# Channel chunks of four neighbours in every twenty, two exponential scales in one operation, and the last output rows on SyncE's queue

## The chip, the core and the metric

The kernel runs on one core of a Trainium2 chip. The core has five engines that run side by side and meet through semaphores: TensorE (PE in the profile; its weight loads are PEld), VectorE (DVE), ScalarE (ACT), GpSimd (POOL) and SyncE (SP), which here only issues transfers. ACT and POOL issue transfers too. The metric is the time on the device in microseconds (us) of one execution, and the median of several runs is compared.

## What is computed

Two independent layers stand side by side in the output (2048 positions, 640 + 640 columns), all in bfloat16.

```python
# A: attention over 8 keys at distances 0, 2, ..., 14; 32 heads of 20 columns
q, k, v = split(x @ wqkv)
a = softmax(scale * q . k[pos - 2 * w]) @ v[pos - 2 * w] @ wo
# B: a state-space layer (S4): 640 channels d, 192 states n, length 2048
dt = exp(log_dt)
P = exp(dt * (A_re + 1j * A_im) * l)                 # (d, n, l)
K = einsum("dn,dnl,dn->dl", C, P, dt * B).real       # one filter per channel
y = irfft(rfft(pad(u)) * rfft(pad(K)))[:2048] + u * Dskip
out = concatenate([a, y], axis=-1)
```

## The kernel before

Part B is built in five chunks of 128 channels (`NCH` = 5, the loop over c in `body`). A partition of a parameter tile stands for a channel of each chunk. The 640 channels are written as four groups g, in each of them 32 rows (u, t) with u of 4 and t of 8, and in each row five neighbours c: channel = 160 g + 40 u + 5 t + c. Chunk c takes every fifth channel. In the tiles that `partB_prep` loads, partition 32 u + 8 g + t holds a row of five channels, one for each chunk. `load` brings each parameter (B_A_re, B_A_im and four more) in with four transfers, one for each u, in which every partition's part is one run of 5 x 192 values. `ldt` is the logarithm of the step, `dtb` its exponential, `dtc` a float32 copy that scales the parameters on DVE. `alpha`, a float32 tile of 192 values for each partition and chunk, is the decay exponent that `decays` makes.

For each chunk, `exps_chunk` makes the powers exp(m x alpha): 14 in RA (m = 1 to 7 and 8 to 56) and 31 in RX (m = 64 to 64 x 31), one ACT operation for each m, and POOL fills the entries with m = 0. `phase_table` makes phases on PE and takes their sines on ACT (tiles TA and TX). `small_half` (L306 in the profile) multiplies powers and phases on DVE into PG, Q and X; `y_form` (L336) makes Y; `kgen_unit` multiplies X and Y on PE (L349 and L354), and one ACT copy (L355) stores eight filter rows in Ksb. A chunk has four such units. `transform` gives the filter's 32 rows of the chunk to `fwd`, a forward transform of length 4096 in two steps, each in four blocks of eight rows: PE (L368), evacuation on ACT (L369), PE (L375), evacuation on ACT (L376). `fwd_u` does the same for the input U, which lies in SBUF as 64 positions x 160 channels for each partition. `products` multiplies the two spectra on DVE (L400), `inverse_a` does half of the inverse (PE L416, ACT L417) and writes to memory (Zdram).

`times_d` (L430) multiplies U by the skip weights Dsb on DVE, 1024 elements at a time, ten times over the loop; the result lies in UD, a tile with one buffer, and POOL issues its transfer to memory (L431). `exps_chunk` is called for the chunk ahead, and `issue_after` queues its ACT operations behind the last sine.

Part A follows while the last chunk ends: projections and logits on PE, products on DVE, a softmax on ACT and DVE. In the last stage the sums over values and the output projection run on PE beside the second half of B's inverse (`Inverse.part`, whose copy writes the channels in order into ysb; SP sends them, L761). `out_piece` makes sixteen pieces of A's output; its transfers (L716) go in turn through POOL and SP, those of the last two pieces through SP. The scheduler of the framework orders the instructions of each engine, except where `keep_in_program_order` or `issue_after` pins them; every engine works its queue in order. The framework adds drains and a barrier at the end (L1061).

Of the kernel before, what the change touches and what calls it, by code (L numbers as in the profile page):

```python
# [16 lines left out]
NCH = 5  # L17
# [78 lines left out]
def partB_prep(tc, pools, prm):  # L96
# [15 lines left out]
    ldt = pl.tile([128, NCH], bf16, name="ldt")  # L112
    lsrc = prm["B_log_dt"].rearrange("(g u t c) -> u g t c", g=4, u=4, t=8)
# [3 lines left out]
    for u in range(4):  # L117
        late((nc.scalar, nc.sync)[u % 2].dma_start(out=ldt[32 * u:32 * u + 32, :], in_=lsrc[u]))
# [3 lines left out]
    def load(nm):  # L122
        nat[nm] = (pl if nm == "B_A_re" else pd).tile([128, NCH, 192], bf16, name=nm, tag=nm)
        src = prm[nm].rearrange("(g u t c) n -> u g t (c n)", g=4, u=4, t=8)
        for u in range(4):
            queue = {"B_A_re": (nc.scalar, nc.sync)[u % 2], "B_A_im": nc.gpsimd, "B_B_im": nc.gpsimd, "B_C_im": nc.gpsimd, "B_C_re": (nc.gpsimd, nc.sync)[u // 2]}.get(nm, nc.sync)
            late(queue.dma_start(out=nat[nm][32 * u:32 * u + 32].rearrange("p c n -> p (c n)"), in_=src[u]))
# [11 lines left out]
    dtb = pl.tile([128, NCH], bf16, name="dtb")  # L139
    late(nc.scalar.activation(out=dtb[:], in_=ldt[:], func=ACT.Exp))  # L140
    dtc = pl.tile([128, NCH], f32, name="dtc")
    V.tensor_copy(out=dtc[:], in_=dtb[:])
# [93 lines left out]
def exps_chunk(tc, pools, B, c):  # L236
    nc = tc.nc
    flat = pools["tab"].tile([128, 9216], bf16, name="R", tag=f"R{c % 2}")
    RA = flat[:, 0:3072].rearrange("p (h g q a f) -> p h g q a f", h=2, g=2, a=8, f=4)
    RX = flat[:, 3072:9216].rearrange("p (q e f) -> p q e f", e=32, f=4)  # L240
    al = B["alpha"][:, c]
    by_half = al.rearrange("p (h v) (q f) -> p h (v q) f", h=2, f=4)
    src = al.rearrange("p u (q f) -> p (u q) f", f=4)
    nc.gpsimd.memset(flat[:, 0:3072].rearrange("p (x a f) -> p x a f", a=8, f=4)[:, :, 0, :], 1.0)
    nc.gpsimd.memset(RX[:, :, 31, :], 1.0)
    for e, m in enumerate(R_MULT):
        if m == 0.0:
            continue
        if e < 16:
            nc.scalar.activation(out=RA[:, :, e // 8, :, e % 8, :], in_=by_half, func=ACT.Exp, scale=m)  # L250
        else:
            nc.scalar.activation(out=RX[:, :, e - 16, :], in_=src, func=ACT.Exp, scale=m)  # L252
    return RA, RX
# [171 lines left out]
def times_d(tc, pools, C, UDd, c, i):  # L425

    nc = tc.nc
    U = C["U"][:].rearrange("p l (ut c) -> p c l ut", c=NCH)[:, c]
    UD = pools["tabb"].tile([128, 32, 32], bf16, name="UD", tag="UD")
    tc.keep_in_program_order(nc.vector.tensor_tensor(out=UD[:], in0=U[:, 32 * i:32 * i + 32], in1=bc(C["Dsb"][:, c], 1, 32), op=A.mult))  # L430
# [3 lines left out]
def fwd_u(tc, pools, C, c, place):  # L434

    U = C["U"][:].rearrange("p l (ut c) -> p c l ut", c=NCH)[:, c]
    return fwd(tc, pools, C, (lambda ut: U[:, :, ut]), 0, pools["fft"], place)

# [5 lines left out]
class Attention:  # L444
# [251 lines left out]
    def out_piece(self, rows, last=False):  # L696
# [4 lines left out]
        whole = self.nop % 2 == 1 and not last  # L701
        self.nop += 1
# [12 lines left out]
        for k in range(ns):  # L715
            (nc.gpsimd, nc.sync)[last or k % 2].dma_start(out=self.out_a[512 * (s0 + k) + i0:512 * (s0 + k) + i0 + ni, :], in_=ob[ni * k:ni * k + ni])  # L716
# [5 lines left out]
class Inverse:  # L722
# [22 lines left out]
    def part(self, half, lo, n):  # L745
# [12 lines left out]
        self.att.copy(out=ysb[:, lo:lo + n].rearrange("p l (ut c) -> p l ut c", c=NCH), in_=ps[:, 0:160 * n].rearrange("p (l c ut) -> p l ut c", l=n, c=NCH))  # L758
# [8 lines left out]
def body(tc, ctx, pools, prm, B_u, B_Dskip, Sd, Zd, UDd, A_x, A_wqkv, A_wo, out_a, out_b):  # L767
# [14 lines left out]
    with tc.tile_pool(name="prep_l", bufs=1) as pl, tc.tile_pool(name="prep_d", bufs=1) as pd, tc.tile_pool(name="prep_g", bufs=1) as pg, tc.tile_pool(name="prep_h", bufs=1) as ph, tc.tile_pool(name="psum_p", bufs=2, space=bass.MemoryType.PSUM) as psp:  # L782
# [22 lines left out]
        nc.gpsimd.tensor_copy(out=Dsb[:], in_=Dn[:].rearrange("p (ut c) -> p c ut", c=NCH))  # L805
# [7 lines left out]
    def transform(c):  # L813
        Sk[c] = fwd(tc, pools, C, (lambda ut: Kb[c][:, ut, :]), 1, fp, "sa" if c == LAST else "ss")[0]
# [251 lines left out]
```

## Time and profile before

| | us |
|---|---|
| runs, median of 3 (lowest to highest) | 410.48 (408.87 to 410.54) |
| the profiled execution, its own time | 406.19 |
| its span, first to last instruction | 404.4 |

The granted TensorE clock of the profiled execution was 0.94 of full speed. A row of a group gives the line, the engine, the operation, the tiles (written from read), their shapes and the count, then the busy time, the mean time of one in nanoseconds, and the idle time of the engine just ahead with what ended it. A row in order of time gives the start, the duration in us, the engine and the same names, and in square brackets the idle time ahead of it. A queue has a q behind the engine's name (SPq).

### The profile page before, as it was taken

What the parts mean: (1) busy time and instruction counts of PE and PEld (TensorE: products, weight loads), DVE (VectorE), ACT (ScalarE), POOL (GpSimd) and SP (SyncE); (2) the same over time, 40 slices, a digit from 0 to 9 for tenths busy, and PEclk for the clock granted to TensorE, in tenths of its full rate; (3) what the DMA queues carried; (4) which work ended last, traced back from release to release, by engine and by line L of the source; (5) the groups of instructions that cost most, each with busy time, mean ns of one, the idle gap of its engine ahead of it and who ended that gap; (6) DMA issues with size and microseconds to landing.
All of it is one profiled execution on the core that took longest, in us unless ns stands there. A gap on an engine that the chain in (4) does not pass through costs nothing.

```text
span 404.4 us, 18790 instructions
## 1 busy us (share of the span) xinstructions
PE 347.6 (86%) x8565; PEld 261.4 (65%) x8565; DVE 369.6 (91%) x350; ACT 311.5 (77%) x572; POOL 58.1 (14%) x116
## 2 busy tenths in 40 slices
PE   1279769989898799987989999999989999779992
PEld 0267668877786788866788666656765677335651
DVE  7999998899998999999999799997967899899960
ACT  2996998789999999999999875633787545856661
POOL 8771000000010000100001000100010030221330
PEclk9975957999999799989998999999999999999997
DMA  5599003032035001440019644300564254697652
GB/s 151 165 233 196 6 3 132 31 74 63 29 131 129 10 6 54 123 118 3 3 60 195 131 99 105 122 11 3 211 162 105 90 146 115 210 248 224 199 137 56
DMA packets 40743, 43.36 MB, mean 107 GB/s; under 512 B 24144, under 2 KB 34096, under 8 KB 40024
## 3 DMA queue, kind: packets, MB, share of 16 engines
q1 hardware_dynamic: 35672, 30.36, 30.1%
q0 software_dynamic: 4848, 11.68, 9.7%
q8 instruction: 67, 1.10, 1.1%
q10 hardware_dynamic: 144, 0.12, 0.1%
q14 instruction: 12, 0.10, 0.1%
HBM read 19.69 MB, written 14.16 MB: 84 GB/s over the span
## 4 chain that ended last, share of the span: by engine, by line
PE 41%; ACT 38%; DVE 11%; issue 4%; DMA 2%; SPq 1%; ACTq 0%; DVEq 0%
ACT R L252 9%; ACT A L369 7%; PE ps_q L545 5%; PE ps_k L527 4%; ACT R L250 4%; PE ps_ph L277 4%; ACT A L376 4%; PE ps_v L558 4%; PE ps_k L349 4%; PE ps_k L354 3%; PE ps_f L375 3%; ACT Z L417 3%; DVE X L306 2%; PE ps_x L461 2%; DVE Y L336 2%
## 5 line engine op out<-in xcount | busy, mean ns | idle before, releaser
L336 DVE TENSOR_TENSOR Y<-PG 128x3072 bf16<-128x3072 bf16 x60 | 103.0, 1754 | 5.3 <-PE ps_k L354 5.3
L349 PE MATMUL ps_k<-Y,X 128*32 128x64 bf16 x1920 | 47.7, 239 | 8.0 <-DVE Y L336 4.1
L277 PE MATMUL ps_ph<-LPB,LPA 128*64 128x256 bf16 x320 | 35.4, 325 | 13.7 <-DMA LPA<-lo 8.2
L349 PEld LDWEIGHTS <-X 128*32 128x32 bf16 x1920 | 32.8, 117 | 18.6 <-issue 9.5
L376 ACT CAST A<-ps_f 128x1024 bf16<-128x1024 f32 x40 | 37.6, 1029 | 6.9 <-PE ps_f L375 6.9
L354 PE MATMUL ps_k<-Y,X 64*32 64x64 bf16 x1920 | 42.1, 233 | 0.0
L252 ACT ACTIVATE R<-LPB 128x192 bf16<-128x192 f32 x155 | 41.7, 377 | 0.0
L369 ACT CAST A<-ps_f 128x1024 bf16<-128x1024 f32 x40 | 37.7, 1040 | 0.6 <-PE ps_f L368 0.6
L306 DVE TENSOR_TENSOR X<-R,TX 128x1536 bf16<-128x1536 bf16 x40 | 37.6, 960 | 0.0
L375 PE MATMUL ps_f<-A,T 128*64 128x128 bf16 x640 | 28.6, 254 | 8.6 <-ACT A L369 8.6
L354 PEld LDWEIGHTS <-X 64*32 64x32 bf16 x1920 | 29.4, 112 | 7.8 <-issue 0.6
L375 PEld LDWEIGHTS <-T 128*64 128x64 bf16 x640 | 26.6, 126 | 10.3 <-issue 9.1
L668 DVE TENSOR_TENSOR prod<-v,atp 128x1536 bf16<-128x1536 bf16 (+3 forms) x32 | 30.8, 1023 | 1.2 <-ACT v L462 1.2
L285 ACT ACTIVATE TX<-ps_ph 128x768 bf16<-128x768 int16 x40 | 30.0, 840 | 0.9 <-PE ps_ph L281 0.7
L277 PEld LDWEIGHTS <-LPA 128*64 128x64 bf16 x320 | 18.4, 125 | 18.3 <-DMA LPA<-hi 8.3
L285 ACT ACTIVATE TA<-ps_ph 128x768 bf16<-128x768 int16 x40 | 29.6, 818 | 0.2
L578 DVE TENSOR_TENSOR prod<-qT,kT 128x1024 bf16<-128x1024 bf16 (+1 forms) x16 | 22.9, 1483 | 4.2 <-ACT qT L546 4.2
L281 PE MATMUL ps_ph<-LPB,LPA 128*64 128x128 bf16 x320 | 24.2, 248 | 0.0
L368 PE MATMUL ps_f<-BD,U 128*64 128x128 bf16 x320 | 20.7, 285 | 2.8 <-ACT Z L417 1.9
L527 PE MATMUL ps_k<-xT,wkq 128*128 128x512 bf16 x100 | 22.9, 379 | 0.2 <-ACT A L376 0.2
L545 PE MATMUL ps_q<-xT,wkq 128*128 128x512 bf16 x100 | 22.6, 379 | 0.0
L368 PEld LDWEIGHTS <-U 128*64 128x64 bf16 x320 | 19.6, 204 | 3.6 <-issue 3.0
(157 smaller groups left out, 719.1 us busy)
## 6 DMA issues: line engine op xcount, KB each, us to landing
P<-A SPq DMA_DIRECT2D x16, 256.0 KB
Zdram<-Z SPq DMA_DIRECT2D x16, 256.0 KB
Z<-Zdram SPq DMA_DIRECT2D x30, 128.0 KB
U<-in_B_u_dram SPq DMA_DIRECT2D x4, 640.0 KB
UDdram<-UD POOLq DMA_DIRECT2D x10, 256.0 KB, 2.8
out_dram<-ysb SPq DMA_DIRECT2D x32, 80.0 KB
Z<-UDdram SPq DMA_DIRECT2D x16, 128.0 KB
Z<-Zdram POOLq DMA_DIRECT2D x10, 128.0 KB, 4.6
```

The costliest lines, as they stand in the source:

```text
L252: nc.scalar.activation(out=RX[:, :, e - 16, :], in_=src, func=ACT.Exp, scale=m)
L277: MM(o[64 * hh:64 * hh + 64, :, 0:8], lhsT=L[:, 64 * hh:64 * hh + 64], rhs=rhs, start=first, stop=last, skip_group_check=True, tile_positi ...
L285: last = nc.scalar.activation(out=dst, in_=words.rearrange("p b (q e f) -> p b q (e f)", e=8, f=4), func=ACT.Sin, scale=PI_LO / 32768.0)
L306: TT = lambda o, a, b, op: V.tensor_tensor(out=o, in0=a, in1=b, op=op)
L336: nc.vector.tensor_tensor(out=Y[:].rearrange("p q (b a) f -> p q b a f", a=8), in0=fa, in1=gb, op=A.mult)
L349: MM(ps[32 * g:32 * g + 32, t], lhsT=X[:, q, k, :, f], rhs=Ys[k][:, q, :, f], start=(t == 0 and k == 0), stop=False, tile_position=(0, 32 ...
L354: MM(ps[32 * g:32 * g + 32, t], lhsT=X[hb, q, k, :, f], rhs=Ys[k][hb, q, :, f], start=False, stop=(k == 2), tile_position=(64 * (g // 2), ...
L368: MM(ps[64 * ri:64 * ri + 64, j], lhsT=src_fn(8 * b + j), rhs=C["BD"][:, wh, ri, :], start=(j % 4 == 0), stop=True, skip_group_check=True, ...
L369: nc.scalar.copy(out=A1[:, 8 * b:8 * b + 8], in_=ps[:])
L375: last = MM(ps[sl, kk], lhsT=C["T2"][:, 8 * b + kk, sl], rhs=A1[:, :, 8 * b + kk, :], start=(kk % 4 == 0), stop=True, skip_group_check=Tru ...
L376: nc.scalar.copy(out=A1[:, :, 8 * b:8 * b + 8, :], in_=ps[:].rearrange("p k (j g) -> p j k g", g=4))
L545: MM(ps[:, i], lhsT=self.wq[:, kt, 128 * ct:128 * ct + 128], rhs=self.x4[:, kt, 2 * i:2 * i + 2, 256 * hf:256 * hf + 256], start=(kt == 0) ...
```

## The change

There are three parts, and what follows from the first.

Chunks. A channel is now 20 p + 4 c + u, with p of 32 for (g, t): a chunk takes four neighbours of every twenty channels, and the four are the four u. The parameters are loaded as five runs of 192 values for each partition, `ldt` brings all twenty steps to a partition, and four copies pick the right ones for `dtc`. U, UD, Dsb and the output copy are addressed by the new order, and the 32 rows n of a chunk's transform are now taken as t = n // 4, u = n % 4, so that row n of the filter is row 8 u + t of Ksb.

Exponentials. For chunks 1 to 4 POOL writes twice alpha over the alpha of the chunk before, so that 2 alpha and alpha lie side by side. An ACT operation over both with scale 64 j then gives the powers 2 j and j. Ten pairs take the place of twenty of the 31 operations of RX, which are made from 31 downward.

Output rows. From piece 11 on all transfers of A's output are issued by SP; pieces 11, 12 and 13 issued two of their four through POOL.

```diff
@@ -109,22 +109,22 @@
     alpha = flat[:, 3616:5536].bitcast(f32).rearrange("p (c u w) -> p c u w", c=NCH, u=4)
     V.memset(early[96:128, :].bitcast(f32), 1.0019378662109375)
     V.memset(flat[96:128, 0:1536].bitcast(f32), 1.0019378662109375)
-    ldt = pl.tile([128, NCH], bf16, name="ldt")
-    lsrc = prm["B_log_dt"].rearrange("(g u t c) -> u g t c", g=4, u=4, t=8)
+    ldt = pl.tile([128, 4 * NCH], bf16, name="ldt")
+    lsrc = prm["B_log_dt"].rearrange("(p x) -> p x", x=4 * NCH)
     late = tc.keep_in_program_order
     one = pl.tile([128, 2], f32, name="one")
     nc.gpsimd.memset(one[:], 0.0)
     for u in range(4):
-        late((nc.scalar, nc.sync)[u % 2].dma_start(out=ldt[32 * u:32 * u + 32, :], in_=lsrc[u]))
+        late((nc.scalar, nc.sync)[u % 2].dma_start(out=ldt[32 * u:32 * u + 32, :], in_=lsrc))
     nat = {}
     F1n, F32n = table_consts_np()
 
     def load(nm):
         nat[nm] = (pl if nm == "B_A_re" else pd).tile([128, NCH, 192], bf16, name=nm, tag=nm)
-        src = prm[nm].rearrange("(g u t c) n -> u g t (c n)", g=4, u=4, t=8)
+        src = prm[nm].rearrange("(p c u) n -> u p c n", c=NCH, u=4)
         for u in range(4):
             queue = {"B_A_re": (nc.scalar, nc.sync)[u % 2], "B_A_im": nc.gpsimd, "B_B_im": nc.gpsimd, "B_C_im": nc.gpsimd, "B_C_re": (nc.gpsimd, nc.sync)[u // 2]}.get(nm, nc.sync)
-            late(queue.dma_start(out=nat[nm][32 * u:32 * u + 32].rearrange("p c n -> p (c n)"), in_=src[u]))
+            late(queue.dma_start(out=nat[nm][32 * u:32 * u + 32], in_=src[u]))
 
     load("B_A_re")
     load("B_A_im")
@@ -136,10 +136,11 @@
     late(nc.scalar.activation(out=one[:], in_=one[:], func=ACT.Exp))
     for nm in ("B_B_re", "B_B_im", "B_C_re", "B_C_im"):
         load(nm)
-    dtb = pl.tile([128, NCH], bf16, name="dtb")
-    late(nc.scalar.activation(out=dtb[:], in_=ldt[:], func=ACT.Exp))
+    dtb = pl.tile([128, NCH, 4], bf16, name="dtb")
+    late(nc.scalar.activation(out=dtb[:].rearrange("p c u -> p (c u)"), in_=ldt[:], func=ACT.Exp))
     dtc = pl.tile([128, NCH], f32, name="dtc")
-    V.tensor_copy(out=dtc[:], in_=dtb[:])
+    for u in range(4):
+        V.tensor_copy(out=dtc[32 * u:32 * u + 32, :], in_=dtb[32 * u:32 * u + 32, :, u])
     dts = pools["fft"].tile([128, NCH], f32, name="dts")
     V.tensor_scalar(out=dts[:], in0=dtc[:], scalar1=4.0 / 3.0, scalar2=None, op0=A.mult)
     id32 = cpool.tile([128, 32], bf16, name="id32", tag="id32")
@@ -243,13 +244,24 @@
     src = al.rearrange("p u (q f) -> p (u q) f", f=4)
     nc.gpsimd.memset(flat[:, 0:3072].rearrange("p (x a f) -> p x a f", a=8, f=4)[:, :, 0, :], 1.0)
     nc.gpsimd.memset(RX[:, :, 31, :], 1.0)
-    for e, m in enumerate(R_MULT):
-        if m == 0.0:
-            continue
-        if e < 16:
-            nc.scalar.activation(out=RA[:, :, e // 8, :, e % 8, :], in_=by_half, func=ACT.Exp, scale=m)
+    if c > 0:
+        twice = B["alpha"][:, c - 1]
+        nc.gpsimd.tensor_tensor(out=twice, in0=al, in1=al, op=A.add)
+        both = B["alpha"][:, c - 1:c + 1]
+        both = both.rearrange("p e u (q f) -> p (u q) e f", f=4)
+    exp = lambda o, i, m: nc.scalar.activation(out=o, in_=i, func=ACT.Exp, scale=m)
+    for e in range(16):
+        if e % 8 > 0:
+            exp(RA[:, :, e // 8, :, e % 8, :], by_half, R_MULT[e])
+    row = lambda k: k - 16 if k > 15 else 31 - k
+    left = list(range(31, 0, -1))
+    while left:
+        k = left.pop(0)
+        if c > 0 and k % 2 == 0 and k // 2 in left:
+            left.remove(k // 2)
+            exp(RX[:, :, row(k):row(k // 2) + 1:row(k // 2) - row(k), :], both, 64.0 * (k // 2))
         else:
-            nc.scalar.activation(out=RX[:, :, e - 16, :], in_=src, func=ACT.Exp, scale=m)
+            exp(RX[:, :, row(k), :], src, 64.0 * k)
     return RA, RX
 
 
@@ -425,16 +437,17 @@
 def times_d(tc, pools, C, UDd, c, i):
 
     nc = tc.nc
-    U = C["U"][:].rearrange("p l (ut c) -> p c l ut", c=NCH)[:, c]
+    U = C["U"][:].rearrange("p l (t c u) -> p c l t u", c=NCH, u=4)[:, c]
     UD = pools["tabb"].tile([128, 32, 32], bf16, name="UD", tag="UD")
-    tc.keep_in_program_order(nc.vector.tensor_tensor(out=UD[:], in0=U[:, 32 * i:32 * i + 32], in1=bc(C["Dsb"][:, c], 1, 32), op=A.mult))
+    by_t = lambda ap: ap.rearrange("p l (t u) -> p l t u", u=4)
+    tc.keep_in_program_order(nc.vector.tensor_tensor(out=by_t(UD[:]), in0=U[:, 32 * i:32 * i + 32], in1=by_t(bc(C["Dsb"][:, c], 1, 32)), op=A.mult))
     nc.gpsimd.dma_start(out=UDd[c, :, 1024 * i:1024 * i + 1024], in_=UD[:].rearrange("p l j -> p (l j)"))
 
 
 def fwd_u(tc, pools, C, c, place):
 
-    U = C["U"][:].rearrange("p l (ut c) -> p c l ut", c=NCH)[:, c]
-    return fwd(tc, pools, C, (lambda ut: U[:, :, ut]), 0, pools["fft"], place)
+    U = C["U"][:].rearrange("p l (t c u) -> p c l t u", c=NCH, u=4)[:, c]
+    return fwd(tc, pools, C, (lambda n: U[:, :, n // 4, n % 4]), 0, pools["fft"], place)
 
 
 S = 2048; D = 640; H = 32; DH = 20; W = 8; DIL = 2; HALO = 14
@@ -699,6 +712,7 @@
         s0, ns, i0, ni = rows
         ob = self.ob[:, self.nop % 6]
         whole = self.nop % 2 == 1 and not last
+        late = self.nop >= 11
         self.nop += 1
         ps = self.more[0][:, :, 0:320]
         for eh in range(2):
@@ -713,7 +727,7 @@
         if whole:
             self.copy(out=ob.rearrange("p (h n) -> p h n", h=2), in_=ps)
         for k in range(ns):
-            (nc.gpsimd, nc.sync)[last or k % 2].dma_start(out=self.out_a[512 * (s0 + k) + i0:512 * (s0 + k) + i0 + ni, :], in_=ob[ni * k:ni * k + ni])
+            (nc.gpsimd, nc.sync)[late or k % 2].dma_start(out=self.out_a[512 * (s0 + k) + i0:512 * (s0 + k) + i0 + ni, :], in_=ob[ni * k:ni * k + ni])
 
     def out_proj(self, some, last=False):
         return [(lambda rows=rows: self.out_piece(rows, last)) for rows in some]
@@ -755,7 +769,7 @@
             for s in range(4) if g0 < g1 else ():
                 i, l = 4 * a + g0 - lo, 4 * s + a0 + a
                 self.att.MM(ps[32 * s:32 * s + 32, 160 * i:160 * (i + g1 - g0)].rearrange("p (g c n) -> p g c n", c=NCH, n=32), lhsT=self.HB[:, 16 * qr + l, :], rhs=self.t[qr][:, g0:g1, :, l, :], start=(i == 0), stop=True, skip_group_check=True, tile_position=(0, 32 * s))
-        self.att.copy(out=ysb[:, lo:lo + n].rearrange("p l (ut c) -> p l ut c", c=NCH), in_=ps[:, 0:160 * n].rearrange("p (l c ut) -> p l ut c", l=n, c=NCH))
+        self.att.copy(out=ysb[:, lo:lo + n].rearrange("p l (t c u) -> p l c t u", c=NCH, u=4), in_=ps[:, 0:160 * n].rearrange("p (l c t u) -> p l c t u", l=n, c=NCH, u=4))
         if lo + n == 8:
             for s in range(4):
                 nc.sync.dma_start(out=self.dst[:, 16 * qr + 4 * s + a0:16 * qr + 4 * s + a0 + 2], in_=ysb[32 * s:32 * s + 32].rearrange("p (a g) n -> p a (g n)", g=4))
@@ -802,7 +816,7 @@
         B["coefficients"](0, psp)
         B["decays"](1, NCH)
         B["weights"](1, NCH)
-        nc.gpsimd.tensor_copy(out=Dsb[:], in_=Dn[:].rearrange("p (ut c) -> p c ut", c=NCH))
+        nc.gpsimd.tensor_copy(out=Dsb[:].rearrange("p c (t u) -> p c t u", u=4), in_=Dn[:].rearrange("p (t c u) -> p c t u", c=NCH, u=4))
     psg = ctx.enter_context(tc.tile_pool(name="psum_g", bufs=2, space=bass.MemoryType.PSUM))
     pools["tabb"] = tabs.enter_context(tc.tile_pool(name="tabb", bufs=1, reuse_waits="tile"))
     pools["tabb"].tile([128, LOW], bf16, name="low")
@@ -811,7 +825,7 @@
     P1 = P2 = None
 
     def transform(c):
-        Sk[c] = fwd(tc, pools, C, (lambda ut: Kb[c][:, ut, :]), 1, fp, "sa" if c == LAST else "ss")[0]
+        Sk[c] = fwd(tc, pools, C, (lambda n: Kb[c][:, 8 * (n % 4) + n // 4, :]), 1, fp, "sa" if c == LAST else "ss")[0]
 
     def spectrum(c):
         P1 = fwd_u(tc, pools, C, c, "sa")[0]
```

## The prediction, made before the change was run

> **What bounds the kernel now.** I read the page's busy times first, then the busy times by stretch, then the chain of waits, then the rows of each engine around the places that the change touches. The page (busy us, share of the span, instructions):
>
> ```profile
> span 404.4 us, 18790 instructions
> PE 347.6 (86%) x8565; PEld 261.4 (65%) x8565; DVE 369.6 (91%) x350; ACT 311.5 (77%) x572; POOL 58.1 (14%) x116
> ```
>
> VectorE (DVE) looks like the bound, but 91% is a mean over stages. The stretches show it stage by stage (start:end, length, then busy time and instruction count of PE, PEld, DVE, ACT and POOL, then granted clock, DMA share, GB/s):
>
> ```profile
> 10.00:28.00 18.00, 8.00 (x95) 6.55 (x95) 17.93 (x36) 17.58 (x53) 14.38 (x26) 0.91 0.79 201
> 75.00:102.00 27.00, 25.18 (x752) 21.48 (x751) 27.00 (x22) 23.88 (x30) 1.10 (x2) 1.00 0.25 62
> 102.00:127.00 25.00, 22.44 (x736) 19.68 (x737) 23.57 (x20) 24.99 (x63) 1.69 (x4) 1.00 0.29 88
> 127.00:155.00 28.00, 24.01 (x747) 20.49 (x736) 27.87 (x23) 26.96 (x50) 1.08 (x2) 0.88 0.14 35
> 155.00:182.00 27.00, 24.77 (x701) 21.09 (x699) 26.24 (x24) 26.12 (x53) 1.71 (x4) 0.94 0.37 107
> 182.00:205.00 23.00, 20.14 (x634) 16.97 (x629) 23.00 (x18) 22.08 (x44) 0.70 (x2) 1.00 0.04 11
> 205.00:230.00 25.00, 22.93 (x653) 19.45 (x651) 22.45 (x19) 24.66 (x49) 1.77 (x2) 0.93 0.63 135
> ```
>
> In the chunk loop (75 to 230 us) two engines are full at once. From 75 to 102 DVE works 27.00 of 27.00 us while ScalarE (ACT) has 3.1 us free; from 102 on ACT is as full as DVE or fuller. Which one ends last at a chunk's boundary is told by DVE's own rows:
>
> ```profile
> 90.70 1.36 DVE L430 TENSOR_TENSOR UD<-U,Dsb 128x1024 bf16<-128x1024 bf16 x1
> 177.00 1.76 DVE L306 TENSOR_TENSOR PG<-R,TA 128x3072 bf16<-128x3072 bf16 x1 [0.76 <-ACT TA L285]
> 226.05 1.76 DVE L306 TENSOR_TENSOR PG<-R,TA 128x3072 bf16<-128x3072 bf16 x1 [2.55 <-ACT TA L285]
> ```
>
> At 177 and 226 us DVE starves 0.76 and 2.55 us for ACT's sines. So up to about 102 us a shorter DVE pays, and after it a shorter ACT pays, not a shorter DVE alone. The change shortens both.
>
> **The U x D product (DVE).** It reads U with neighbours five channels apart; afterwards it reads runs of four. The group rows, with a product of the same 1024 elements whose operands are contiguous:
>
> ```profile
> L430 DVE TENSOR_TENSOR UD<-U,Dsb 128x1024 bf16<-128x1024 bf16 x10 | 13.5, 1348 | 0.0
> L578 DVE TENSOR_TENSOR prod<-qT,kT 128x1024 bf16<-128x1024 bf16 x10 | 6.4, 681 | 4.2 <-ACT qT L546 4.2
> L306 DVE TENSOR_TENSOR Q<-PG,cT 128x3072 bf16<-128x3072 bf16 x10 | 17.9, 1785 | 0.1
> ```
>
> Q, which also runs in fours, takes 1785 ns for 3072 elements, 0.58 ns each; contiguous takes 681/1024 = 0.67. So runs of four are as quick as contiguous data, and UD goes from 1348 to about 681 ns: 0.67 us each, 6.7 us for ten. Lower end: nothing, if the three-dimensional walk is not streamed in pairs.
>
> **Exponentials (ACT).** Of 31 operations per chunk in RX, ten pairs (30 with 15, 28 with 14, down to 16 with 8, then 6 with 3 and 4 with 2) become one operation each in chunks 1 to 4: 40 fewer, each twice as long. Back-to-back runs give the price:
>
> ```profile
> 13.23 7.93 ACT L252 ACTIVATE R<-LPB 128x192 bf16<-128x192 f32 x31
> 22.48 2.92 ACT L285 ACTIVATE TA<-ps_ph 128x768 bf16<-128x768 int16 x4
> ```
>
> 192 elements cost 7.93/31 = 0.256 us, 768 cost 2.92/4 = 0.730. By a straight line 384 cost 0.414, against 0.512 for two singles: 0.098 us saved per pair, 3.9 us in all, 0.98 per chunk. Lower end 0, if two interleaved scales read slower than a straight row; no row shows that walk.
>
> **The doubled exponents (GpSimd).** `twice` adds one 192-element float32 sum per chunk on POOL. It writes the alpha of the chunk before, so it waits for that chunk's last exponential, and the DMAs of UD queue behind it on POOL. Its price has two nearby rows, a copy of 160 and one of 280 elements, and what stood beside the first on DVE:
>
> ```profile
> 31.04 0.36 POOL L805 COPY Dsb<-Dn 128x160 bf16<-128x160 bf16 x1
> 259.48 0.82 POOL L538 COPY kT<-kT 128x280 bf16<-128x280 bf16 x1
> 31.00 2.04 DVE L306 TENSOR_TENSOR Q<-PG,cT 128x3072 bf16<-128x3072 bf16 x1
> ```
>
> The Q beside POOL's copy took 2.04 us against 1.785 in the mean: DVE lost 0.25. The Trainium skill, "SBUF — State Buffer", section "SBUF: two separate sides", says that a GpSimd operation and a VectorE operation with two SBUF inputs shut each other out for a whole instruction, which speaks against the change; this row agrees in direction, losing less than the copy's 0.36. I take 0.25 us of DVE for each of four, 1.0 in all (0 to 3.3, the latter if each shuts DVE out for 0.82).
>
> **The order of the filter's rows.** Before, block b of eight rows of the forward transform of K came from unit b alone, so it could start before the last unit was copied out of PSUM. Now each block takes rows from all four units:
>
> ```profile
> 181.44 0.58 ACT L355 CAST Ksb<-ps_k 128x512 bf16<-128x512 f32 x1 [0.50 <-PE ps_k L354]
> 182.00 2.84 ACT L369 CAST A<-ps_f 128x1024 bf16<-128x1024 f32 x3
> 181.32 1.53 PE L368 MATMUL ps_f<-BD,Ksb 128*64 128x128 bf16 x48
> ```
>
> Before, PE's first 48 matmuls began at 181.32, ahead of the last copy (181.44 to 182.02), and ACT's evacuations followed it at once. Now the first block can start only at 182.02; 16 matmuls take 1.53/3 = 0.5 us and ACT waits that long plus a hand-over, 0.7 us. This hits the transforms of chunks 0, 1 and 2 (those of 3 and 4 come long after their units). The first lies in the stretch where ACT has 3.1 us free; so 2 x 0.7 = 1.4 us count. From 0, if other evacuations fill the gap, to 2.7 (3 x 0.9).
>
> **The middle's sum.** Up to 102 us DVE sets the pace: three products (the one before PG at about 74, then 90.70 and 101) give 3 x 0.67 = 2.0, less 0.3 for `twice`. After it ACT sets the pace: three chunks of exponentials, 2.9, less 1.4 for the transforms. Together -1.7 - 1.5 = -3.2 us. The rest of UD's saving vanishes in waits for ACT. If the gaps are filled and both engines shorten together, it is at most -6.7.
>
> **The last output rows.** Pieces 11, 12 and 13 each send two of four DMAs from POOL; these six move to SyncE (SP). The last piece on POOL is then number 10. Rows of the end: the drains, SP's issues (min/median/max ns), then POOL's and SP's issues in time:
>
> ```profile
> L1061 SPq DRAIN x2: 7/10/12, 400.3 to 400.4; - x2
> L1061 POOLq DRAIN x1: 8073/8073/8073, 395.6 to 395.6; - x1
> L716 SPq DMA_DIRECT2D out_dram<-ob x16: 314/414/595, 382.8 to 397.9; - x16
> 388.89 0.99 POOL L716 DMA_DIRECT2D out_dram<-ob  x2 [3.25 <-ACT ob L462]
> 391.38 0.98 POOL L716 DMA_DIRECT2D out_dram<-ob  x2 [1.50 <-ACT ob L462]
> 393.01 0.98 POOL L716 DMA_DIRECT2D out_dram<-ob  x2 [0.65 <-ACT ob L462]
> 395.15 0.98 POOL L716 DMA_DIRECT2D out_dram<-ob  x2 [1.16 <-ACT ob L462]
> 396.04 2.47 SPq L716 DMA_DIRECT2D out_dram<-ob  x4
> ```
>
> SP has seen every output land and drains at 400.3, but POOL's drain, begun at its last DMA, ends at 395.6 + 8.07 = 403.7, and the program ends 0.7 later. POOL holds the end by 3.3 us. If the drain is tied to POOL's last DMA, it now starts at about 389.4 and ends at 397.5, out of the way. SP then sets the end, and pays for six more issues at about 0.46 us with their gap: piece 11 from 391.1 to 393.0, piece 12 to 394.8, piece 13 (ready at about 394.9) to 396.7, piece 14 (two) to 398.0, piece 15 to 399.1, where it now ends at 396.04 + 2.47 = 398.5. So SP drains 0.6 later, at 400.9, and the span ends at 401.7: -2.7 us. Ends: +0.6 (POOL's drain stays late, SP's issues count) and -3.3.
>
> **The start.** Every parameter row splits from one piece of 1920 B into five of 384, and `dtc` needs four copies instead of one.
>
> ```profile
> 3.61 5.39 DMA B_A_re<-in_B_A_re_dram
> 9.68 3.65 ACT R L250 x14
> 5.75 0.17 DVE L142 CAST dtc<-dtb 128x5 f32<-128x5 bf16 x1 [0.67 <-ACT dtb L140]
> LPA<-hi POOLq DMA_DIRECT2D x2, 24.0 KB, 4.1
> ```
>
> The last quarter of A_re takes 5.39 us and lands at 9.00; ACT's exponentials begin at 9.68. A transfer in pieces of 384 B (LPA<-hi, two on POOL) takes 4.1 us at its median, so small pieces alone need not be later. The Trainium skill, "DMA: Bandwidth & Descriptors", pulls both ways. Its section "Specifications" wants at least 512 B per piece for the full rate, against the change. Its section "Why a DMA increments its semaphore by 16 and not by 1" says that the slowest dimension sets how many of the 16 DMA engines a transfer uses: 4 of them by the old view (g=4), 16 by the new one (32 rows), for the change. No row here separates the two. I take A_re as no later. The three extra copies put 3 x 0.17 = 0.5 us on DVE, which then works 17.93 of 18 us; 0.3 of it is given back by shorter waits for parameters, as an estimate: +0.2 us (-0.6 to +2.7, if A_re took half as long again).
>
> The output copies of `Inverse.part` (same elements on ACT) and Dsb's copy I cost at nothing: ACT and POOL do the same count, and neither ends last there.
>
> **Sum.** -3.2 - 2.7 + 0.2 = -5.7 us. The profiled execution, 404.4 us of span and 406.19 in all, would become 398.7 and 400.5. The median of the runs, 410.48, lies 4.3 above the profiled execution; taking the same difference from it gives 404.8.
>
> **Rivals.** *More overlap* (chance 0.13): both engines shorten together and the start gains 0.6: -6.7 - 2.7 - 0.6 = -10, 400.5. Against it stand the 0.76 and 2.55 us for which DVE already waits.
>
> *The drain stays* (0.12): POOL's 8.07 us have another cause and end where they did. Then -3.2 + 0.6 + 0.2 = -2.4, 408.1. For it: the trace has only one such drain.
>
> *Small pieces are late* (0.12): by the rule of 512 B, A_re lands 2.7 us later, and everything follows it. The middle and the tail still give 5.9: -3.2, 407.3; if B's and C's loads also hold DVE by as much, -0.5, 410.0. No row shows a load of this kind slow.
>
> *POOL's queue blocks DVE* (0.14), slower. UD has a single buffer, so DVE's next UD waits for the DMA of the last one to land. That DMA stands in POOL's queue, where `twice` may stand ahead of it, waiting for the end of the previous chunk's exponentials:
>
> ```profile
> 119.63 0.54 POOL L431 DMA_DIRECT2D UDdram<-UD  x1 [6.72 <-DVE UD L430]
> 125.77 1.36 DVE L430 TENSOR_TENSOR UD<-U,Dsb 128x1024 bf16<-128x1024 bf16 x1
> 120.87 6.75 ACT L252 ACTIVATE R<-LPB 128x192 bf16<-128x192 f32 x26
> DMA to landing us min/median/max: 2.3/2.8/5.6
> ```
>
> If `twice` of chunk 3 is queued ahead of the DMA of 119.63, it waits until 127.6; the DMA goes out at 128.2 and lands at 131.0, and DVE, in order, loses 131.0 - 125.8 = 5.2 us, here and, by as much, one chunk later. With two such stalls (10.4) less the gains (5.7) the time is +4.7, 415.2; with one, -0.5. It decides when `twice` stands ahead of UD's DMA by over 5 us. Against it: POOL is idle for long stretches in which the sum could go.
>
> **Chances.** Forecast 0.49, rivals 0.13, 0.12, 0.12, 0.14. Half a per cent, 2.05 us, is about what a measurement of this kernel can tell from no change: below 408.4 is faster, above 412.5 slower. Faster: 0.49 + 0.13, half of the drain's case and half of the small pieces' case, 0.74, less 0.04 for orders of the instructions that no row shows: 0.70. Slower: two stalls, 0.10, and 0.04 of the same: 0.14. The rest, 0.16, is the same. The range for 8 in 10 runs from the overlapping case, 400.5, to one stall or late loads, 411.0.
>
> **What would show it.** UD at about 0.68 us; 21 exponentials in RX for chunks 1 to 4; ACT's first evacuation after a K transform about 0.7 us after the last Ksb copy; POOL's drain ending ahead of SP's and the end within 1 us of SP's drain; A_re landing at or before 9 us. The forecast is wrong if POOL's drain still ends 3 us after SP's, if DVE shows waits ahead of UD, or if ACT's idle time in the loop grows by more than the exponentials save.

## The result, and the profile after

The changed kernel is slower: the ratio of its time to the kernel before is 1.0072, with a 95% interval of 1.0044 to 1.0100. Its median is 411.72 us against 409.45 of the runs beside it; in us the ratio is +3.0. The forecast was 5.7 us faster. Ratios here and below leave out executions more than 1.5% above the fastest of their kernel; in e4, e11 and e12 these are three or four of twelve, at 425.9 to 430.2 us, and why is open.

The profiled execution has a span of 409.6 us (411.44 in all). One thing must be known before the two traces are laid side by side. The profiled execution of the kernel before, at 406.19, lies 4 us below the median of its runs, and one place where it differs is the granted clock in the last stage. The first row is the kernel before, the second the changed one (columns as in the prediction's table by stretch):

```profile
350.00:375.00 25.00, 20.64 (x508) 11.12 (x508) 24.58 (x26) 14.96 (x29) 6.57 (x12) 1.00 0.82 233
```

```profile
354.00:379.00 25.00, 22.63 (x481) 10.03 (x481) 23.04 (x24) 13.68 (x26) 6.02 (x11) 0.73 0.79 221
```

With 0.73 granted instead of 1.00, 481 instead of 508 matmuls (PE's count) lie in these 25 us. This does not go with the change: between 350 and 375 us most experiments below show 0.73 to 0.80, among them e3, which has the kernel before's layout, and e2 (the old layout) and e7 (the new one) show 1.00. So places in the traces are compared up to 250 us and within the last few us, and ends are compared by the ratios of many runs alone.

The page after (busy us, share of the span, instructions):

```profile
span 409.6 us, 18756 instructions
PE 347.6 (85%) x8565; PEld 256.8 (63%) x8565; DVE 364.9 (89%) x353; ACT 307.9 (75%) x532; POOL 70.0 (17%) x114
```

DVE has 4.7 us less to do than before and ACT 3.6 us less, and neither shows in the time. The groups that answer to the prediction's (idle time just ahead and its cause at the right):

```profile
L443 DVE TENSOR_TENSOR UD<-U,Dsb 128x1024 bf16<-128x1024 bf16 x10 | 6.9, 686 | 0.3 <-DMA UDdram<-UD 0.3
L252 ACT ACTIVATE R<-LPB 128x192 bf16<-128x192 f32 (+1 forms) x185 | 56.5, 400 | 0.1
L381 ACT CAST A<-ps_f 128x1024 bf16<-128x1024 f32 x40 | 37.7, 1032 | 2.3 <-PE ps_f L380 2.3
```

UD takes 686 ns (681 forecast). The exponentials are 40 fewer and take 56.5 us instead of 41.7 + 18.9 = 60.6 in the two old groups, which are the first two rows below. Two new waits matter in what follows. The smaller one is the third row above: ACT waits 2.3 us for PE ahead of the first evacuations of the transforms, and before the change 0.6 (the last row below):

```profile
L252 ACT ACTIVATE R<-LPB 128x192 bf16<-128x192 f32 x155 | 41.7, 377 | 0.0
L250 ACT ACTIVATE R<-LPB 128x192 bf16<-128x192 f32 x70 | 18.9, 353 | 0.1
L369 ACT CAST A<-ps_f 128x1024 bf16<-128x1024 f32 x40 | 37.7, 1040 | 0.6 <-PE ps_f L368 0.6
```

The larger one no part of the prediction had. In order of time, POOL's copy and DVE's first product PG:

```profile
33.50 0.33 POOL L819 COPY Dsb<-Dn 128x160 bf16<-128x160 bf16 x1
33.87 1.76 DVE L318 TENSOR_TENSOR PG<-R,TA 128x3072 bf16<-128x3072 bf16 x1 [5.18 <-POOL Dsb L819]
```

Before, PG began at 28.46 while the copy was still to come (31.04). Now it waits 5.18 us for a copy whose result it does not read. ACT then waits in its turn, for DVE's X, ahead of the sines TX (0.9 us in all before; 2.2 in e1 below, where PG is not late):

```profile
L297 ACT ACTIVATE TX<-ps_ph 128x768 bf16<-128x768 int16 x40 | 29.7, 834 | 6.8 <-DVE X L318 5.8 <-PE ps_ph L293 0.9
```

The next places at which DVE lost or gave back time, and the end:

```profile
99.47 2.29 DVE L412 TENSOR_TENSOR A<-A,A 128x4096 bf16<-128x4096 bf16 x1 [2.21 <-DMA P<-A]
178.43 1.76 DVE L318 TENSOR_TENSOR PG<-R,TA 128x3072 bf16<-128x3072 bf16 x1 [1.31 <-ACT TA L297]
227.30 1.76 DVE L318 TENSOR_TENSOR PG<-R,TA 128x3072 bf16<-128x3072 bf16 x1 [2.77 <-ACT TA L297]
246.38 3.43 DVE L348 TENSOR_TENSOR Y<-PG 128x3072 bf16<-128x3072 bf16 x2 [1.96 <-PE ps_k L366]
250.59 1.75 DVE L318 TENSOR_TENSOR PG<-R,TA 128x3072 bf16<-128x3072 bf16 x1
403.22 0.49 DVE L707 CAST ob<-ps_o 128x320 bf16<-128x320 f32 x1 [0.87 <-PE ps_o L474]
```

```profile
L1075 POOLq DRAIN  x3: 46/102/7585, 395.7 to 409.3; - x3
L1075 SPq DRAIN  x3: 7/7/13, 408.7 to 409.0; - x3
```

PG is 5.4 us late at 33.87, and only 1.4 and 1.25 at 178.43 and 227.30: UD and the exponentials did give time back. Then DVE waits for PE at 246.38, and the last such PG, at 250.59, is 3.3 us late again (247.29 before). At the end POOL's long drain, 7.585 us from 395.7, is over at 403.3, and SP's at 408.7 sets the end, 5.0 us after DVE's last operation (403.22 + 0.49).

### The profile page after: what moved, and what is told of

Read it like the earlier page. It is cut to its first block, busy times and chain, and to the rows that moved or that the text cites. A ratio compares the mean times of both kernels' runs of the same rounds, so it can differ in the third digit from the quotient of the medians.

```text
span 409.6 us, 18756 instructions
## 1 busy us (share of the span) xinstructions
PE 347.6 (85%) x8565; PEld 256.8 (63%) x8565; DVE 364.9 (89%) x353; ACT 307.9 (75%) x532; POOL 70.0 (17%) x114
## 4 chain that ended last, share of the span: by engine, by line
PE 50%; ACT 34%; DVE 6%; DMA 5%; issue 2%; SPq 1%; ACTq 0%; POOL 0%; DVEq 0%
ACT R L252 9%; ACT A L381 8%; PE ps_k L540 6%; PE ps_k L361 5%; ACT A L388 5%; PE ps_k L366 5%; PE ps_ph L289 5%; PE ps_q L558 5%; PE ps_v L571 4%; PE ps_f L387 3%; PE ps_x L474 3%; PE ps_o L474 3%; PE ps_op L474 3%; DMA U<-in_B_u_dram 3%; ACT Z L429 2%
## 5 line engine op out<-in xcount | busy, mean ns | idle before, releaser
L252 ACT ACTIVATE R<-LPB 128x192 bf16<-128x192 f32 (+1 forms) x185 | 56.5, 400 | 0.1
L289 PE MATMUL ps_ph<-LPB,LPA 128*64 128x256 bf16 x320 | 32.2, 301 | 16.3 <-DMA LPA<-lo 6.6
L289 PEld LDWEIGHTS <-LPA 128*64 128x64 bf16 x320 | 17.0, 116 | 21.5 <-issue 17.9
L318 DVE TENSOR_TENSOR PG<-R,TA 128x3072 bf16<-128x3072 bf16 x10 | 17.5, 1753 | 9.3 <-POOL Dsb L819 5.2
L293 PE MATMUL ps_ph<-LPB,LPA 128*64 128x128 bf16 x320 | 22.5, 234 | 0.0
L380 PE MATMUL ps_f<-BD,U 128*64 128x128 bf16 x320 | 20.4, 284 | 1.0 <-ACT Z L429 0.8
```

What stands on the lines that cost most here:

```text
L252: exp = lambda o, i, m: nc.scalar.activation(out=o, in_=i, func=ACT.Exp, scale=m)
L289: MM(o[64 * hh:64 * hh + 64, :, 0:8], lhsT=L[:, 64 * hh:64 * hh + 64], rhs=rhs, start=first, stop=last, skip_group_check=True, tile_positi ...
L318: TT = lambda o, a, b, op: V.tensor_tensor(out=o, in0=a, in1=b, op=op)
```

## The experiments

Ratios are to the kernel before, each with its 95% interval; 0.001 is 0.41 us.

**The late PG.** PG's memory comes from a pool that is laid over the one of the preparation (`prep_l`), and a placeholder `low` of `LOW` = 1344 bfloat16 values, 2688 bytes, keeps the tiles behind it off that memory. Counted from the code, with each tile rounded up to a multiple of 32 bytes (an assumption on the layout), `prep_l` held exactly 2688 bytes: 32 + 32 (ldt) + 1920 + 32 (dtb) + 32 + 320 + 320 (Dn, the last). The change makes ldt and dtb 40 bytes long, 64 each, so 2752. Then Dn ends 64 bytes behind `low`, under PG, and PG must wait until POOL has read it.

```diff
 e1, on the changed kernel          e2, on the kernel before
-LOW = 1344                         -LOW = 1344
+LOW = 1376                         +LOW = 1312
```

> The changed kernel with the placeholder tile `low` 64 bytes longer; the instructions of every engine and their order are the same, only addresses differ. Theory 'overlap' (the wider ldt and dtb push Dn 64 bytes past the placeholder, so that the first PG lies on Dn's memory and must wait until POOL has copied it to Dsb): the first PG begins at 28.2 to 29 us instead of 33.87, no wait for Dsb stands ahead of it, the span is 3 to 5 us shorter than the changed kernel's 409.6, so 405 to 407, and the time is between 0.993 and 1.001 of the kernel before. Rival 'order' (PG is late because the new loads and the new order of PE and POOL make its inputs late, and Dsb is only what the profile names): the first PG still begins after 33 us and the time stays at 1.007.

> The kernel before with the placeholder tile `low` 64 bytes shorter, so that its PG lies over the end of Dn as in the changed kernel; same instructions, same order. Theory 'overlap': the first PG waits for POOL's copy of Dsb (31.04 + 0.36) and begins at 31.5 to 32 instead of 28.46, a loss of 3.0 us at that place; the later chunk boundaries give some of it back, so the time is 1 to 3 us (0.2 to 0.7%) above the kernel before. Rival 'order': nothing changes, PG at 28.5, ratio 1.000.

Measured: e1 0.9953 (0.9920 to 0.9985), e2 1.0106 (1.0052 to 1.0160). The same place in e1, then in e2:

```profile
28.21 1.75 DVE L318 TENSOR_TENSOR PG<-R,TA 128x3072 bf16<-128x3072 bf16 x1
```

```profile
32.44 1.76 DVE L306 TENSOR_TENSOR PG<-R,TA 128x3072 bf16<-128x3072 bf16 x1 [3.53 <-POOL Dsb L805]
```

Sixty-four bytes, with not one instruction moved, take the wait from the changed kernel and put it into the kernel before. They are worth 1.0072 - 0.9953, 4.9 us, in the one and 4.3 us in the other, each uncertain by about 2, so a stall at 28 us is hardly given back: e2 had expected 1 to 3. This is shown. With it mended the change gains 1.9 us, not the 5.7 forecast, so more is missing.

**The output rows alone,** on the kernel before:

```diff
 e3; in out_piece
+        late = self.nop >= 11
-            (nc.gpsimd, nc.sync)[last or k % 2].dma_start(...)
+            (nc.gpsimd, nc.sync)[late or k % 2].dma_start(...)
```

> The kernel before with the third part of the change alone: output rows from piece 11 on all issued by SP. By the prediction: POOL's drain (8.07 us from POOL's last transfer) ends at about 397.5, SP drains 0.6 later than before, the span ends 2.7 us earlier, ratio 0.993. Rival 'SP's queue': SP's issues get slower when they stand back to back (over 1 us for some, as the changed kernel's trace shows twice), SP drains 3 to 4 us later than before, and the span moves by -1 to +1, ratio 0.998 to 1.002.

Measured: 0.9965 (0.9932 to 0.9998), -1.4 us, between the two. SP's issues and the drains, and DVE's last operation:

```profile
L717 SPq DMA_DIRECT2D out_dram<-ob x22: 315/419/1767, 386.6 to 404.3; - x22
L1062 POOLq DRAIN  x3: 46/102/7588, 393.1 to 407.4; - x3
L1062 SPq DRAIN  x3: 7/7/13, 406.8 to 407.1; - x3
400.64 0.49 DVE L694 CAST ob<-ps_o 128x320 bf16<-128x320 f32 x1 [0.87 <-DMA out_dram<-ob]
```

POOL's drain is out of the way (393.1 + 7.6 = 400.7), as forecast. But SP drains 406.8 - 401.1 = 5.7 us after DVE's last operation. In the kernel before this was 3.0 (drain at 400.3, and the row below), and one issue now lasts 1.767 us where the longest was 0.595.

```profile
396.84 0.49 DVE L694 CAST ob<-ps_o 128x320 bf16<-128x320 f32 x1 [0.87 <-DMA out_dram<-ob]
```

So SP pays some 2 us or more for its six further issues instead of 0.6. Two attempts to relieve it, on e1's kernel:

```diff
 e5
-        late = self.nop >= 11
+        late = self.nop >= 12
 e6, on e5
-        late = self.nop >= 12
+        late, final = self.nop >= 12, self.nop == 15
-            (nc.gpsimd, nc.sync)[late or k % 2].dma_start(...)
+            (nc.scalar if final and k % 2 == 0 else (nc.gpsimd, nc.sync)[late or k % 2]).dma_start(...)
```

> The changed kernel with `low` at 1376, and SP taking all rows from piece 12 on instead of piece 11. Theory 'SP's queue' (SP's issues of the last pieces stand back to back and end 3 us after the last copy, while POOL has long drained): two issues less on SP (0.42 each with their gap, and perhaps one of the long ones of 1.5), POOL's drain ends at about 402, still ahead of SP's; the end comes 0.9 to 2 us sooner than with piece 11, ratio to the kernel before 0.990 to 0.994. Rival 'landing' (the end is set by the transfers themselves, not by their issue): same as with piece 11, 0.995.

> As e5_low1376_from12, and half of the last piece's transfers are issued by ACT, which has nothing else left to do. Theory 'SP's queue': one or two issues of about 0.6 us each leave the end of SP's queue, so the end comes 0.6 us sooner than in e5. Rival 'landing': no change, or the end comes later because ACT's transfer starts from another queue.

Measured: e5 0.9962 (0.9926 to 0.9998), e6 0.9954 (0.9923 to 0.9985), both like e1's 0.9953. The end of e5:

```profile
399.51 0.49 DVE L707 CAST ob<-ps_o 128x320 bf16<-128x320 f32 x1 [0.87 <-PE ps_o L474]
L1075 SPq DRAIN  x3: 7/7/13, 404.2 to 404.5; - x3
```

SP drains 4.2 us after DVE's last operation, in e6 as well, and 5.0 us after it in e1 (404.3 and 398.81). So two issues fewer on SP save 0.8 us in the trace, a little less than the 0.9 to 2 expected and too little for these ratios, each uncertain by 1.3 to 1.5 us, to tell. Moving half of the last piece to ACT saves nothing more.

**The exponentials alone,** on the kernel before: e4 has the second part of the change's diff as it is, with the doubled exponents made by POOL; in e11 DVE makes those of chunks 2 to 4.

```diff
 e11; e7 likewise, on e5
-        nc.gpsimd.tensor_tensor(out=twice, in0=al, in1=al, op=A.add)
+        (nc.gpsimd if c == 1 else nc.vector).tensor_tensor(out=twice, in0=al, in1=al, op=A.add)
```

> The kernel before with the second part of the change alone: in chunks 1 to 4 POOL doubles alpha and ten pairs of exponentials become one operation each. By the prediction: ACT's exponentials take 3.9 us less in all (0.98 per chunk), of which 2.9 count from 102 us on, less 0.3 for the doubled exponents: -2.6 us, ratio 0.994. Rival 'no room' (DVE, PE or the granted clock is late where ACT gets shorter): ACT's busy time falls by 4 us and its idle time grows by as much, ratio 0.998 to 1.001. Rival 'POOL' (the doubling sits in POOL's queue ahead of UD's transfers): DVE shows waits for a UD transfer, 1.005 or more.

> The kernel before with the paired exponentials as in e4_before_exps, but the doubled exponents of chunks 2, 3 and 4 made by DVE. Theory 'shut out' (in e4 POOL's sum waited 30.5 us for a gap of DVE, UD's transfer waited behind it and DVE then waited 2.65 us for UD): no such wait, the exponentials bring the 2.6 us that were forecast, ratio 0.992 to 0.995. Rival 'no room': ratio 0.998 to 1.001 as in e4.

> As e5_low1376_from12, and the doubled exponents of chunks 2, 3 and 4 are made by DVE instead of POOL. Theory 'shut out' (POOL's sum of 192 values cannot start while DVE's operations follow each other without a gap; it took 13.6 us in one place and 30.5 in another, and UD's transfer stood behind it): no POOL operation is longer than 1.5 us, UD's transfer of chunk 1 goes out right after its UD instead of at 69.7, DVE pays three sums of about 0.25 us; the time is within 1 us of e5, a little faster if a wait of DVE for UD went away. Rival 'POOL's own' (the sum is long by itself): DVE's sums are long as well.

Measured: e4 0.9994 (0.9960 to 1.0029), e11 0.9960 (0.9928 to 0.9991), e7 0.9952 (0.9916 to 0.9987). POOL and DVE in e4:

```profile
170.19 30.51 POOL L248 TENSOR_TENSOR LPB<-LPB 128x192 f32<-128x192 f32 x1
200.65 0.56 POOL L442 DMA_DIRECT2D UDdram<-UD  x1
195.25 5.08 DVE L347 TENSOR_TENSOR Y<-PG 128x3072 bf16<-128x3072 bf16 x3
202.98 1.31 DVE L441 TENSOR_TENSOR UD<-U,Dsb 128x1024 bf16<-128x1024 bf16 x1 [2.65 <-DMA UDdram<-UD]
```

A sum of 192 values is on POOL for 30.51 us. DVE runs without a gap until 195.25 + 5.08 = 200.33, where its next UD must wait for the transfer of the last one; the sum ends at 200.70, and only then does the transfer behind it go out. In the changed kernel one such sum takes 13.58 us, and e1 shows it at 55.62 with 13.57. On DVE the same sum takes 0.35 (e7). The intervals of e4 and e11 overlap, so the gain from the move is not beyond doubt; but the wait of 2.65 us is gone in e11, and its gain of 1.6 us is nearer the forecast of 2.6. In the changed kernel the sums happen to fall where UD can wait, and e7 is not measurably faster than e5.

**The layout alone,** and the order of the filter's rows. e8 is the changed kernel with `low` at 1376 and with the exponentials and the output rows of the kernel before. In e9, e10, e13, e14 and e16 each block of the filter's first step takes the rows of one unit again, and ACT's evacuation puts them where the new order needs them; e15 does the reverse to the kernel before.

```diff
 e9 (on e7), e13 (on e8), e14 (on e1), e16 (on the changed kernel); in fwd, for the filter only
-MM(..., lhsT=Kb[c][:, 8 * (n % 4) + n // 4, :], ...)        # n = 8 * b + j
+MM(..., lhsT=Kb[c][:, n, :], ...)
-nc.scalar.copy(out=A1[:, 8 * b:8 * b + 8], in_=ps[:])
+nc.scalar.copy(out=A1[:].rearrange("p (t u) k g -> p u t k g", u=4)[:, b], in_=ps[:])
```

> The first part of the change alone (chunks of four neighbours) with `low` at 1376; exponentials and output rows as before. By the prediction: UD's 2.0 us up to 102 us, less 1.4 for the wait of the filter's transforms, plus 0.2 at the start: -0.4 us, ratio 0.999. Theory 'transfer chain': DVE reaches the product A<-A,A 2 us sooner and waits there as long for the last transfer P<-A, so that nothing is left at 102 us; ratio 0.998 to 1.002. If UD's 6.7 us counted in full: 0.985.

> The first part of the change alone with `low` at 1376, as e8_low1376_layout_only (1.0062), and the filter's rows taken unit by unit. Theory 'row order' (the 2.5 us that the layout alone costs are the waits of ACT at the start of the filter's transforms): ACT's idle time there falls from 2.6 to under 1 us, ratio 0.997 to 1.001. Rival 'elsewhere' (the loss comes from UD's earlier transfers, the phases on PE or the tail): 1.004 to 1.007.

> The whole change with two mends only: `low` at 1376 and the filter's rows taken unit by unit (doubled exponents on POOL, rows from piece 11 on SP). If the mends add up: e1's 0.9953 less what row order costs, 0.986 to 0.991, as e9's 0.987; the forecast of 5.7 us less would be 0.986. If e9 owed its time to DVE's doubled exponents and not to the row order: 0.994 to 0.997.

> The changed kernel with the filter's rows taken unit by unit and nothing else altered; `low` stays at 1344, so the first PG still waits for Dsb. If row order costs 3.8 to 4.7 us here too: 1.0072 less 0.0093 to 0.0115, so 0.996 to 0.998; if it costs the 1.4 us forecast: 1.004. PG's wait of 5.2 us for Dsb stays in either case.

> As e7_low1376_twice_dve, and the first step of the filter's transform takes the rows of Ksb unit by unit, as before the change; ACT's evacuation puts them into the places of the new order. Theory 'row order' (the new layout alone costs 2.5 us because ACT, which is full from 127 us on, waits for PE at the start of three filter transforms): ACT's idle time ahead of the first evacuations falls from 2.3 to under 1 us, ACT reaches the sines of the last chunk 1.5 to 2.5 us sooner, ratio 0.989 to 0.992 where e7 had 0.995. Rival 'PE' (the wait is taken up by PE's phases a little later): ACT's idle time moves from the evacuations to the sines, ratio 0.994 to 0.996.

Measured, without and with the order mended: the layout alone e8 1.0062 (1.0034 to 1.0090), e13 0.9947 (0.9915 to 0.9979); the whole change with `low` mended e1 0.9953, e14 0.9860 (0.9814 to 0.9906); the change as it is 1.0072, e16 0.9998 (0.9960 to 1.0036); with the sums on DVE e7 0.9952, e9 0.9874 (0.9829 to 0.9918). Four pairs: 4.7, 3.8, 3.0 and 3.2 us, each uncertain by about 2; the two of a pair were not run side by side, but each beside the kernel before. ACT's evacuations in e8, then in e13:

```profile
L370 ACT CAST A<-ps_f 128x1024 bf16<-128x1024 f32 x40 | 37.6, 1031 | 2.6 <-PE ps_f L369 2.6
```

```profile
L371 ACT CAST A<-ps_f 128x1024 bf16<-128x1024 f32 x40 | 37.6, 1032 | 0.7 <-PE ps_f L369 0.7
```

The wait that goes is 1.9 us; the time that goes is 3 to 4.7. The traces do not show where the rest goes. The last PG begins at 248.55 in e8 and 248.49 in e13, at 246.28 in e1 and 246.80 in e14, at 250.59 in the changed kernel and 246.69 in e16, at 248.52 in e7 and 245.51 in e9: two pairs show nothing up to there, two show 3.9 and 3.0 us. Single executions scatter: e1, e5 and e6, which differ only in their last output rows, have this PG at 246.28, 246.65 and 247.69. So the size rests on the ratios alone. And the reverse, on the kernel before:

> The kernel before, in which the first step of the filter's transform takes the rows of Ksb in the changed order (each block of eight from all four units) and ACT's evacuation puts them back into their old places. Nothing else is changed. Theory 'row order, as forecast' (0.7 us of ACT at each of three transforms, of which two count): +1.4 us, ratio 1.003. Theory 'row order, more' (e8 against e13 and e1 against e14 say 3.8 to 4.7 us, the wait of ACT being only a part): ratio 1.007 to 1.012. Rival (the gain of e13 and e14 came from something other than the order of the rows): 1.000.

Measured: 0.9993 (0.9962 to 1.0025). Its evacuations of the filter wait as long as e8's:

```profile
L370 ACT CAST A<-ps_f 128x1024 bf16<-128x1024 f32 x20 | 18.8, 1029 | 1.9 <-PE ps_f L368 1.9
```

So the same 1.9 us of ACT's waiting cost at most 1 us in the kernel before, where DVE has 6.6 us more to do with UD, and 3 us or more in the new layout. That DVE's longer UD covered the wait is the reading that fits; it is argued, not shown, and why the new layout pays more than the wait itself is open.

**The chain of transfers.** In the row at 99.47 above DVE waits for the last of four transfers P<-A, each of which is issued when the one before has landed. e8 shows the same wait without the exponentials or the tail:

```profile
95.09 2.29 DVE L401 TENSOR_TENSOR A<-A,A 128x4096 bf16<-128x4096 bf16 x1 [2.48 <-DMA P<-A]
```

The transfers copy the spectrum of U, which the product then overwrites. In the changed kernel, ACT's last evacuations of U's transform, SP's four issues, and ACT's last evacuations of the filter's transform:

```profile
82.21 3.76 ACT L388 CAST A<-ps_f 128x1024 bf16<-128x1024 f32 x4 [1.08 <-PE ps_f L387]
86.00 10.94 SPq L395 DMA_DIRECT2D P<-A  x4
92.14 3.76 ACT L388 CAST A<-ps_f 128x1024 bf16<-128x1024 f32 x4 [0.90 <-PE ps_f L387]
```

The transfers start when U's transform is done (85.97). The filter's transform is done at 95.90, before DVE comes to the product at 97.26 (99.47 less 2.21). So the order of the filter's rows has no part in this wait, and where it is mended the wait stays: 2.94 us in e13, 2.37 in e16.

```diff
 e10, on e9; in swapped
-for n in range(0, 4096, wide)], after, wide < 4096)
+for n in range(0, 4096, wide)], after, False)
```

> As e9_unit_order, and the four transfers P<-A of a chunk no longer wait for each other's landing. Theory 'transfer chain' (DVE waits 2.3 to 2.9 us at the product A<-A,A of chunk 0 for the last of four transfers in a row, which is where UD's saving goes): that wait falls below 1 us and PG of chunk 1, second half, begins 1.5 to 2.5 us sooner. Whether the end gains by it is open: ACT is full from there on, so 0 to 1.5 us, ratio 0.987 to 0.992. Rival: the transfers together take as long as one after the other, and the wait stays.

Measured: the wait is gone, PG of chunk 1 begins at 98.87 where e9 has 99.55, and the ratio is 0.9954 (0.9923 to 0.9985), 3.3 us worse than e9 (uncertain by 2.2). DVE's wait for PE a little later, 2.45 us in e9, ahead of a Y that begins there at 119.71, is longer:

```profile
120.31 3.43 DVE L348 TENSOR_TENSOR Y<-PG 128x3072 bf16<-128x3072 bf16 x2 [3.72 <-PE ps_k L366]
```

So the 0.7 us that DVE is ahead at 98.87 are lost 20 us later. Why the end is even later was not settled.

**Without the layout:** the exponentials (sums on DVE) and the output rows on the kernel before.

> As e11_before_exps_dve, and the output rows from piece 11 on all issued by SP: the second and third part of the change without the first. If the parts add up: e11's ratio less e3's 0.0035, so 0.989 to 0.991 by theory 'shut out', 0.995 to 0.997 by 'no room'.

Measured: 0.9937 (0.9902 to 0.9971); e11 and e3 add up to 0.9925. The best version is the whole change with both mends, e14 at 0.9860 and e9 at 0.9874, 5.2 to 5.7 us faster than the kernel before, each uncertain by about 1.9: roughly what was forecast for the change as it stands. That the numbers meet is chance: the forecast took off 1.4 us for the order of the rows, which these two versions do not pay, and its sum without that term is -7.1.

## Why the prediction was wrong, step by step

*The missing step: where the tiles lie.* The sum costed every instruction that the change touches and no address. `ldt` and `dtb` grew by 30 bytes each, PG's memory came to lie over Dn, and DVE stalled 5.18 us at 33.87. Undone in e1, copied in e2: 4.3 to 4.9 us. The part called "the start" gave +0.2.

*The term that was too small: the order of the rows.* The mechanism was right. After the last Ksb copy ACT waits 0.56 us in the changed kernel (0.7 forecast), for PE's first block, at three transforms. The size was wrong by the ratios: 1.4 us were put down, and four pairs of runs say 3 to 4.7. ACT's own waits are no larger than forecast, so what the rest is made of stays open. It is not the first transform, which the prediction let go free: that one is done 1.4 us before DVE asks for it.

*The middle: "DVE sets the pace".* The sum booked 2.0 us of UD's saving up to 102 us. DVE does come to the product A<-A,A sooner, but no term had the transfers P<-A that it must then wait for, 2.21 us in the changed kernel and none before. In e8 the PG that began at 102.60 begins at 101.78, so 0.8 of the 2.0 us are left, and in e13 it begins at 103.03. e10 takes the wait away, and PE is next.

*The output rows.* POOL's drain is tied to its last transfer, as forecast, and left the end, which is 0.8 to 0.9 us after SP's drain (0.7 forecast). The term for SP was too small: 0.6 us were put down, 2 to 2.7 measured. Single issues of up to 1.77 us are part of it; how much was not separated. So -1.4 instead of -2.7, uncertain by 1.4.

*The exponentials.* 4.1 us less of ACT (3.9 forecast). Alone they gave 1.6 us of the 2.6 with DVE's sums, and about nothing with POOL's. The price of the doubled exponents was sought on DVE (0.25 us each); it lies on POOL, which gets no turn. The rival "POOL's queue blocks DVE" named the place and the victim, UD's single buffer, but another cause: not a wait for ACT, but DVE itself. In the changed kernel it cost 0.32 us, in e4 2.65. Of the signs that the prediction named for being wrong, this wait ahead of UD came, and ACT's idle time from the first PG to the last grew from 20.4 to 24.7 us, about as much as the exponentials save.

*Right:* UD at 686 ns, 21 exponentials in RX, and the start. A_re is no later in pieces of 384 bytes but earlier; the last quarter's first weights on PE, before and after:

```profile
9.04 0.10 PEld L157 LDWEIGHTS <-B_A_re 32*128 32x128 bf16 x1 [1.10 <-DMA B_A_re<-in_B_A_re_dram]
```

```profile
7.70 0.10 PEld L158 LDWEIGHTS <-B_A_re 32*128 32x128 bf16 x1
```

It no longer waits for the transfer. This agrees with the Trainium skill, "DMA: Bandwidth & Descriptors", section "Why a DMA increments its semaphore by 16 and not by 1": the slowest dimension is now 32 rows instead of 4 groups, and by that section more engines share the transfer, which no row here counts. The rule of 512 bytes in its section "Specifications" shows no loss here. With the row order mended the layout alone is worth -2.2 us (e13), where the prediction's terms without that order give -2.0 + 0.2; but e13's trace does not have it where the forecast put it, before 102 us, so the agreement is luck as far as is known.

## What to carry to other kernels

When a change makes a tile larger, even by 30 bytes, ask which later tile comes to lie on its memory and which slow engine reads it last: a wait for a tensor that the instruction does not use is the sign of it. When rows are renumbered, let the consumer take them in the order in which they are produced and let a copy that is made anyway put them in place. And follow time that an engine saves to the next thing that it waits for: what DVE saved up to 102 us went mostly into a wait for transfers that no term of the sum had.

## What the runs showed of the hardware

A GpSimd sum of 192 values took 0.5 to 3.2 us in most places, and 13.6 (e1) and 30.5 us (e4) where DVE's operations followed each other without a gap; on DVE it took 0.35. Both long ones ended some 0.4 us after DVE's run did: 69.19 against 68.83, and 200.70 against 200.33. The Trainium skill, "SBUF — State Buffer", section "SBUF: two separate sides", has the two engines shut each other out for the length of an instruction. Here it was the length of DVE's whole unbroken run.

POOL's drain at the end, which begins with its last transfer, lasts 7.6 to 8.1 us in all these runs, though it begins anywhere from 390.7 to 400.7 us.
